# A decode block that streams a KV cache: transposed PV, an aligned load ring, an earlier wo half and a shorter ending

## The chip, the cores and the metric

The kernel runs on one core of a Trainium2 chip. The metric is device time in microseconds, the median over several executions. Ratios are the mean time of one kernel's runs over that of the kernel before in the same rounds, so they are not quite the ratio of the medians quoted.

## The reference

One token passes through an adaLN-conditioned block: modulation from `c`, a layer norm, attention with a cached K and V (32 query heads, 8 KV heads, 32768 positions, head size 128), an output projection, a second layer norm, and a ReLU MLP.

```python
mod = (_silu(c) @ w_mod).reshape(c.shape[0], 6, 1, -1)
sa, ca, ga, sb, cb, gb = ...
h = _layernorm(x) * (1 + ca) + sa
q = (h @ wq)...;  scores = q . k * Dh**-0.5;  p = softmax(scores);  o = p @ v
x = x + ga * (o.reshape(B, Sq, Hq * Dh) @ wo)
h = _layernorm(x) * (1 + cb) + sb
x = x + gb * (jnp.maximum(h @ w1, 0) @ w2)
```

K and V are 134 MB of the 149.4 MB that the kernel must read, so it is a streaming problem: nothing is used twice.

## The kernel before

All large inputs come through one ring of eight 16 KB slots a partition, on one DMA queue, in a fixed order. Each load of 2 MB is 128 packets of 16 KB (the trace has 8704 of them for 68 such loads), and its semaphore counts to 16. The completion records show sixteen separate increments, and the page counts 16 DMA engines, so each increment is read here as the end of one engine's share of the load. The ring follows the pool of constants in memory.

```python
    const = ctx.enter_context(tc.tile_pool(name="const", bufs=1))
    ring = ctx.enter_context(tc.tile_pool(name="ring", bufs=8))
    ktpool = ctx.enter_context(tc.tile_pool(name="ktpool", bufs=3))
    spool = ctx.enter_context(tc.tile_pool(name="spool", bufs=2))
...
    stream = [("wm", 0), ("wm", 1), ("wq", 0), ("wq", 1)]
    stream += [("k", 0, u) for u in range(NTILE)]
    for g in range(Hkv):
        for u in range(NTILE):
            if g + 1 < Hkv:
                stream.append(("k", g + 1, u))
            stream.append(("v", g, u))
    stream += [("wo", b) for b in range(NHALF)]
    stream += [("w1",), ("w2a",), ("w2b",)]
```

PV holds a slice of the probabilities stationary and streams V, 16 matmuls of 512 columns for each 2 MB tile. It leaves four partial sums side by side, which `gather` adds up.

```python
    def pv(g, u):
        if u == 0:
            o_tiles[g] = ps_o.tile([16, 4 * Dh], F32, tag="o", name="o_ps")
        o_ps, PT_g = o_tiles[g], PT_tiles[g]
        Vsb = need(("v", g, u))
        G, s0 = u // 2, 4 * (u % 2)
        for j in range(16):
            c0 = (16 * G + j) * 32 + 4 * s0
            nc.tensor.matmul(
                o_ps[:], lhsT=PT_g[:, c0:c0 + 16],
                rhs=Vsb[:].rearrange("p (s j) d -> p s j d", j=16)[:, :, j, :],
                start=(u == 0 and j == 0), stop=(u == NTILE - 1 and j == 15),
            )

    def gather(g):

        b, gl = divmod(g, GH)
        X = spool.tile([16, 4 * Dh], F32, tag="X", name="X")
        nc.scalar.copy(out=X[:], in_=o_tiles.pop(g)[:])
        for s in range(4):
            nc.tensor.matmul(
                acc[b][:, 0:Dh], lhsT=osel[:, gl, s, :], rhs=X[:, s * Dh:(s + 1) * Dh],
                start=False, stop=(gl == GH - 1 and s == 3), skip_group_check=True,
            )
```

The layer norm works on a transposed vector (128 x 4). Its middle is a matmul with ones that sums over partitions (0.59 us in the ending's timeline).

```python
    def layernorm_T(src_T, dst_T, shiftT, scaleT, tagp):
        stat_in = const.tile([P, 2], F32, name=f"stat_in_{tagp}")
        junk = const.tile([P, KT], F32, name=f"junk_{tagp}")
        nc.vector.tensor_scalar(
            out=junk[:], in0=src_T, scalar1=1.0 / D, scalar2=None,
            op0=ALU.mult, op1=ALU.add, accum_out=stat_in[:, 0:1],
        )
        nc.vector.scalar_tensor_tensor(
            out=junk[:], in0=src_T, scalar=1.0 / D, in1=src_T,
            op0=ALU.mult, op1=ALU.mult, accum_out=stat_in[:, 1:2],
        )
        stat_ps = small_ps([P, 2], f"stat_ps_{tagp}")
        nc.tensor.matmul(stat_ps[:], lhsT=ones_f[:], rhs=stat_in[:], start=True, stop=True)
        st = const.tile([P, 2], F32, name=f"st_{tagp}")
        nc.vector.tensor_copy(out=st[:], in_=stat_ps[:])
        negvar = const.tile([P, 1], F32, name=f"negvar_{tagp}")
        nc.vector.scalar_tensor_tensor(
            out=negvar[:], in0=st[:, 0:1], scalar=st[:, 0:1], in1=st[:, 1:2],
            op0=ALU.mult, op1=ALU.subtract,
        )
        std = const.tile([P, 1], F32, name=f"std_{tagp}")
        nc.scalar.activation(out=std[:], in_=negvar[:], func=ACT.Sqrt, bias=eps_t[:], scale=-1.0)
        rstd = const.tile([P, 1], F32, name=f"rstd_{tagp}")
        nc.vector.reciprocal(out=rstd[:], in_=std[:])
        xn = const.tile([P, KT], F32, name=f"xn_{tagp}")
        nc.vector.tensor_scalar(
            out=xn[:], in0=src_T, scalar1=st[:, 0:1], scalar2=rstd[:],
            op0=ALU.subtract, op1=ALU.mult,
        )
        t1 = const.tile([P, KT], F32, name=f"t1_{tagp}")
        nc.vector.scalar_tensor_tensor(
            out=t1[:], in0=scaleT, scalar=1.0, in1=xn[:], op0=ALU.add, op1=ALU.mult,
        )
        nc.vector.tensor_tensor(out=dst_T, in0=t1[:], in1=shiftT, op=ALU.add)
```

The main loop and the ending. `project(b)` multiplies by one half of wo (2 MB each, 64 matmuls of one column). `rows4` turns the residual `x1` into row form with 16 small fp32 matmuls (32 passes in the profile, 1.16 us) and a copy on VectorE (0.29 us); `normalise(b)` forms `o2` out of four heads' groups.

```python
    build_qbd(0)
    for u in range(NTILE):
        scores(0, u)
    softmax(0)
    for g in range(Hkv):
        if g + 1 < Hkv:
            build_qbd(g + 1)
        for u in range(NTILE):
            if g + 1 < Hkv:
                scores(g + 1, u)
            pv(g, u)
        PT_tiles.pop(g)
        if g + 1 < Hkv:
            softmax(g + 1)
        gather(g)
        if g % GH == GH - 1:
            normalise(g // GH)
    for b in range(NHALF):
        project(b)
...
    x1T = const.tile([P, KT], F32)
    nc.vector.tensor_tensor(out=x1T[:], in0=attnT_ps[:], in1=modT_sb[:, 2 * KT:3 * KT], op=ALU.mult)
    nc.vector.tensor_tensor(out=x1T[:], in0=x1T[:], in1=xT[:], op=ALU.add)
    h2T = const.tile([P, KT], BF16)
    layernorm_T(x1T[:], h2T[:], modT_sb[:, 3 * KT:4 * KT], modT_sb[:, 4 * KT:5 * KT], "ln2")

    x1_rows = rows4(x1T[:], "x1_rows")

    w1_sb = need(("w1",))
    w1_f = w1_sb[:].rearrange("p kt (a m b) -> p kt a b m", m=P, b=FB)
    ...  # 56 matmuls with w1 into hidT_ps
    hidT = const.tile([P, FT], BF16)
    nc.scalar.activation(out=hidT[:], in_=hidT_ps[:], func=ACT.Relu)
    ffn_ps = small_ps([P, P], "ffn_ps")
    nc.vector.memset(ffn_ps[:], 0.0)
    for part, base, n in (("w2a", 0, FA - 1), ("w2b", FA - 1, 1)):
        w2_sb = need((part,))
        for a in range(n):
            for b in range(FB):
                ft = (base + a) * FB + b
                for i in range(KT):
                    nc.tensor.matmul(
                        ffn_ps[32 * i:32 * i + 1, :], lhsT=hidT[:, ft:ft + 1],
                        rhs=w2_sb[:, a, b, i * P:(i + 1) * P], start=False, stop=(ft == FT - 1),
                        skip_group_check=True,
                    )
```

## Time and profile before

| | value | where read |
|---|---|---|
| time | 362.34 us (361.85 to 362.76), the three runs that the prediction had; 362.1 us with a fourth in the rounds of the result | runs |
| profiled span | 360.1 us | page |
| PE, PE weight loads, VectorE busy | 79%, 34%, 50% | page, part 1 |
| DMA rate, middle slices | 420 to 435 GB/s | page, part 2 |
| step from one landing of a 2 MB tile to the next | 4.894 us | completion records in the trace |

The page of the kernel before: its DMA rows, one digit or number for each fortieth of the span, then its DMA queues (packets, MB, share of the 16 engines' span) and the chain of waits that ended last.

```profile
DMA  8999999999999999999999999999999999999992
GB/s 302 428 430 430 431 423 426 428 431 426 426 431 428 428 424 431 428 426 430 428 427 428 431 421 428 431 424 428 431 430 424 426 435 420 430 431 428 424 404 92
...
q1 hardware_dynamic: 11160, 149.43, 98.0%
q8 instruction: 13, 0.21, 0.2%
...
DMA 86%; DVE 6%; issue 5%; PE 2%; DVEq 0%
```

The stream never pauses between the first slice and the last two. Note q8: the page calls its kind "instruction", and its 13 packets are read here as the fetching of the program itself. The completion records below show that it takes time from the engines that carry the data, about 1.5 us a packet.

The table of DMA issues says how long after its issue a load landed (columns: transfer, queue, count, KB, median us).

```profile
Vsb<-in_A_v_cache_dram SPq DMA_DIRECT2D x32, 2048.0 KB, 33.9
```

A load lands 33.9 us after issue and a tile takes 4.9 us, so about seven loads are always queued. A slot freed earlier buys nothing (with the ring aligned, the step was 4.862 us with the old PV in run 3 and 4.864 us with the new); only the rate of the stream, and what comes after its end, count.

PV in the groups of instructions (engine, operation, shape, count, then busy us and mean ns of one, then idle time before it):

```profile
L371 PE MATMUL o_ps<-Vsb,PT_g 128*16 128x512 bf16 x512 | 117.9, 385 | 1.1 <-DVE PT_g L352 1.0
```

The end of the kernel, from the timeline (start us, duration us, engine, line, operation, count, and in brackets the idle time before and what ended it):

```profile
346.75 2.29 PE L414 MATMUL attnT_ps<-o_sb,wo_sb 128*128 128x1 bf16 x64 [1.36 <-DMA wo_sb<-in_A_wo_dram]
...
350.97 0.29 ACT L202 ACTIVATE std_ln<-negvar_ln,eps_t 128x1 f32<-128x1 f32 x1 [8.58 <-DVE negvar_ln L197]
...
351.61 0.29 DVE L250 COPY x_rows_sb<-x_rows_ps 128x128 f32<-128x128 f32 x1 [0.67 <-PE x_rows_ps L245]
351.82 0.15 DVE L204 RECIPROCAL rstd_ln<-std_ln 128x1 f32<-128x1 f32 x1
...
352.75 1.63 PE L455 MATMUL hidT_ps<-h2T,w_sb 128*128 128x1 bf16 x56 [1.17 <-DVE h2T L214]
...
355.01 1.45 PE L469 MATMUL ffn_ps<-w2a_sb,hidT 128*1 128x128 bf16 x48 [0.63 <-DMA w2a_sb<-in_B_w_dram]
356.25 0.43 PE L469 MATMUL ffn_ps<-w2b_sb,hidT 128*1 128x128 bf16 x8
```

wo's second half waited for its DMA; the matmuls of w2 waited for theirs.

The page shows only the last of a transfer's sixteen increments. The trace has all; these are the sixteen times (us, sorted) of the last load, w2's last piece, in the kernel before:

```
352.1 352.2 352.3 352.4 352.6 352.8 353.0 353.7 353.9 353.9 354.0 354.1 355.3 355.3 355.4 355.5
```

The engines finish 3.4 us apart, in three groups 1.4 us apart: seven, five and four engines. The records of the loads before it, laid beside the packets of the instruction queues, show how this came about. After each packet of q8, in that load or the next, one engine and only one falls back by about 1.5 us, and it stays back. These are two loads around the packet at 60.5 us (landing of the fastest engine, then how far behind it each engine is, sorted; us):

```
59.2  0.0 0.2 0.2 0.2 0.3 0.3 0.4 0.4 0.4 0.5 0.5 0.6 0.6 1.2 1.9 2.0
64.1  0.0 0.2 0.2 0.2 0.3 0.3 0.4 0.4 0.4 0.5 0.6 0.6 1.2 2.0 2.0 2.1
```

An engine that was about 0.5 us behind is now 2.1 us behind. Twelve of the 13 packets were sent before the stream ended. The first eight hit eight different engines that were up with the rest; the next four hit engines that had been hit once. That makes four engines with one fetch and four with two. The fifth engine of the middle group had none: two of the four 8 KB packets of q14 (at 50.4 and 297.3 us) are each followed by a step of about 1.0 us on an engine that ends in this group.

### The profile page before, as it was taken

The numbers are of one execution on the slowest core, as the hardware profiler recorded it, in microseconds if no ns is written. First come the engines' busy times: TensorE is split into PE (matmuls) and PEld (weight loads), VectorE is DVE, ScalarE is ACT, GpSimd is POOL, SyncE is SP. The second block draws the span as 40 slices with busy tenths as digits, with TensorE's granted clock in tenths as the row PEclk, the third lists the DMA queues.
The fourth block names the chain that finished last, engine by engine and source line by source line (L and its number), as shares of the span: only waits on it lengthen the run. The fifth ranks groups of instructions, "written<-read, shape, count | busy, mean of one in ns | idle before, by whom it ended". The sixth has DMA issues, their size and how long they took to land.

```text
span 360.1 us, 3889 instructions
## 1 busy us (share of the span) xinstructions
PE 283.2 (79%) x1680; PEld 123.2 (34%) x1680; DVE 180.3 (50%) x193; ACT 31.6 (9%) x73; POOL 9.4 (3%) x15
## 2 busy tenths in 40 slices
PE   0547876987997889777977889886976799788964
PEld 0542332433333334323332323333432333333363
DVE  2239976555644465556554474446555474431021
ACT  1022012003000110003000300012000200011100
POOL 9100000000000000000000000000000000000000
PEclk9999998999699989989999989989998869999965
DMA  8999999999999999999999999999999999999992
GB/s 302 428 430 430 431 423 426 428 431 426 426 431 428 428 424 431 428 426 430 428 427 428 431 421 428 431 424 428 431 430 424 426 435 420 430 431 428 424 404 92
DMA packets 11465, 149.68 MB, mean 416 GB/s; under 512 B 1464, under 2 KB 1464, under 8 KB 2360
## 3 DMA queue, kind: packets, MB, share of 16 engines
q1 hardware_dynamic: 11160, 149.43, 98.0%
q8 instruction: 13, 0.21, 0.2%
q10 hardware_dynamic: 288, 0.00, 0.0%
q14 instruction: 4, 0.03, 0.0%
HBM read 149.42 MB, written 0.00 MB: 415 GB/s over the span
## 4 chain that ended last, share of the span: by engine, by line
DMA 86%; DVE 6%; issue 5%; PE 2%; DVEq 0%
DMA Ksb<-in_A_k_cache_dram 76%; DMA w2a_sb<-in_B_w_dram 9%; DVE KTt L305 6%; DMA xc_bf<-in_c_dram 2%; PE o_ps L371 1%; PE S_ps L314 1%; PE ffn_ps L469 0%; DVE S_g L320 0%; DVE o_rows L475 0%; DVE o_bf L477 0%; DVEq L305 0%; PE mT_ps L330 0%
## 5 line engine op out<-in xcount | busy, mean ns | idle before, releaser
L305 DVE STREAM_TRANSPOSE KTt<-Ksb 128x2048 f32<-128x2048 f32 x64 | 144.5, 2287 | 61.2 <-DMA Ksb<-in_A_k_cache_dram 61.2
L314 PE MATMUL S_ps<-KTt,qbd 128*128 128x512 bf16 x512 | 133.7, 411 | 34.4 <-DVE KTt L305 33.5
L371 PE MATMUL o_ps<-Vsb,PT_g 128*16 128x512 bf16 x512 | 117.9, 385 | 1.1 <-DVE PT_g L352 1.0
L314 PEld LDWEIGHTS <-qbd 128*128 128x128 bf16 x512 | 51.2, 103 | 111.8 <-issue 67.8
L371 PEld LDWEIGHTS <-PT_g 128*16 128x16 bf16 x512 | 44.2, 91 | 72.5 <-issue 15.5
L320 DVE TENSOR_SCALAR_CACHE_REDUCE S_g<-S_ps 128x512 f32<-128x512 f32 x16 | 11.0, 686 | 42.4 <-PE S_ps L314 42.4
L284 ACT COPY qbd<-qrep_sb 32x128 bf16<-32x128 bf16 x32 | 9.4, 295 | 179.5 <-PE S_ps L314 178.4
L381 ACT COPY X<-o_ps 16x512 f32<-16x512 f32 x8 | 4.6, 575 | 100.3 <-PE o_ps L371 100.3
L231 PE MATMUL modT_ps<-siluT,wm_sb 128*128 128x1 bf16 x96 | 3.3, 172 | 12.3 <-DVE siluT L223 12.3
L332 DVE TENSOR_REDUCE Mrow<-mT_ps 1x4 f32<-1x128 f32 x8 | 2.2, 279 | 20.6 <-PE mT_ps L330 20.6
L352 DVE STREAM_TRANSPOSE PT_g<-P_g 128x1024 bf16<-128x1024 bf16 x8 | 9.7, 1211 | 5.4 <-ACT P_g L347 5.3
L383 PE MATMUL oh_ps<-X,osel 16*16 16x128 f32 x64 | 10.2, 305 | 1.1 <-ACT X L381 1.1
L358 PE MATMUL oh_ps<-l_g,lsel 128*16 128x1 f32 x16 | 1.6, 171 | 11.4 <-ACT P_g L347 11.4
L347 ACT ACTIVATE P_g<-S_g,nbias 128x1024 bf16<-128x1024 f32 x8 | 9.2, 1148 | 0.4 <-ACT nbias L344 0.2
L394 DVE RECIPROCAL linv<-oh_ps 16x1 f32<-16x1 f32 x2 | 0.3, 134 | 15.8 <-PE oh_ps L383 15.8
L231 PEld LDWEIGHTS <-wm_sb 128*128 128x128 bf16 x96 | 3.4, 118 | 12.1 <-DMA wm_sb<-in_w_mod_dram 7.2
L262 PE MATMUL qT_ps<-hT,wq_sb 128*128 128x1 bf16 x128 | 3.7, 165 | 4.3 <-DVE hT L214 3.4
L383 PEld LDWEIGHTS oh_ps<-X,osel 16*16 16x16 f32 x64 | 5.8, 102 | 3.4 <-ACT X L381 1.8
L342 PE MATMUL Mb_ps<-ident_f,Mexp 1*128 1x1 f32 x16 | 3.0, 256 | 3.7 <-DVE Mexp L337 3.7
L414 PE MATMUL attnT_ps<-o_sb,wo_sb 128*128 128x1 bf16 x128 | 4.6, 172 | 1.4 <-DMA wo_sb<-in_A_wo_dram 1.4
L358 PEld LDWEIGHTS oh_ps<-l_g,lsel 128*16 128x16 f32 x16 | 0.9, 97 | 12.6 <-ACT P_g L347 9.7
L262 PEld LDWEIGHTS <-wq_sb 128*128 128x128 bf16 x128 | 3.6, 104 | 4.4 <-issue 3.5
(86 smaller groups left out, 60.3 us busy)
## 6 DMA issues: line engine op xcount, KB each, us to landing
Ksb<-in_A_k_cache_dram SPq DMA_DIRECT2D x32, 2048.0 KB, 34.0
Vsb<-in_A_v_cache_dram SPq DMA_DIRECT2D x32, 2048.0 KB, 33.9
wq_sb<-in_A_wq_dram SPq DMA_DIRECT2D x2, 2048.0 KB, 17.1
wo_sb<-in_A_wo_dram SPq DMA_DIRECT2D x2, 2048.0 KB, 34.2
wm_sb<-in_w_mod_dram SPq DMA_DIRECT2D x2, 1536.0 KB, 6.4
w_sb<-in_B_w_dram SPq DMA_DIRECT2D x1, 1792.0 KB, 34.0
w2a_sb<-in_B_w_dram SPq DMA_DIRECT2D x1, 1536.0 KB, 32.4
w2b_sb<-in_B_w_dram SPq DMA_DIRECT2D x1, 256.0 KB, 25.4
```

The lines of the kernel that those rows point to most:

```text
L231: nc.tensor.matmul(modT_ps[:, j * KT + ko:j * KT + ko + 1], lhsT=lhsT[:, ko, :], rhs=siluT[:, kt:kt + 1], start=(kt == 0), stop=(kt == KT ...
L262: nc.tensor.matmul(qT_ps[:, hq:hq + 1], lhsT=wq_sb[kt // 2][:, kt % 2, hq * Dh:(hq + 1) * Dh], rhs=hT[:, kt:kt + 1], start=(kt == 0), stop ...
L284: nc.scalar.copy(out=o, in_=i)
L305: nc.vector.transpose(out=KTt[:].bitcast(F32), in_=Ksb[:, 32 * half:32 * half + 32, :].rearrange("p j d -> p (j d)").bitcast(F32),)
L314: nc.tensor.matmul(S_ps[:], lhsT=qbd[g % 2][:, hp, s, :], rhs=KTv[:, 16 * sl:16 * sl + 16, h, :, par], start=(t4 == 0 and sl == 0 and hp = ...
L320: nc.vector.tensor_scalar(out=S_tiles[g][:, G, :], in0=S_ps[:], scalar1=1.0, scalar2=None, op0=ALU.mult, op1=ALU.max, accum_out=m_tiles[g] ...
L347: nc.scalar.activation(out=P_g[:], in_=S_g[:].rearrange("p g f -> p (g f)"), func=ACT.Exp, bias=nbias[:], scale=scale, accum_out=l_g[:],)
L352: nc.vector.transpose(out=PT_g[:], in_=P_g[:])
L371: nc.tensor.matmul(o_ps[:], lhsT=PT_g[:, c0:c0 + 16], rhs=Vsb[:].rearrange("p (s j) d -> p s j d", j=16)[:, :, j, :], start=(u == 0 and j ...
L381: nc.scalar.copy(out=X[:], in_=o_tiles.pop(g)[:])
L383: nc.tensor.matmul(acc[b][:, 0:Dh], lhsT=osel[:, gl, s, :], rhs=X[:, s * Dh:(s + 1) * Dh], start=False, stop=(gl == GH - 1 and s == 3), sk ...
L414: nc.tensor.matmul(attnT_ps[:, ko:ko + 1], lhsT=wo_sb[:, r, :].rearrange("p (m ko) -> p ko m", ko=KT)[:, ko, :], rhs=o2[:, r:r + 1], start ...
```

## The change

Its intent, part by part: hold V stationary so that PV's result comes out transposed and needs no gathering (four times as many matmuls, each of 4 columns); start the ring at a multiple of 256 bytes; load and use wo's first half ahead of the last V; shorten the norm; split w2 in three so that little work follows the last landing; and make the x1 rows after w1's matmuls.

The diff, cut to its core:

```diff
+
+    front = ctx.enter_context(tc.tile_pool(name="front", bufs=1))
+    mask4 = front.tile([P, 32], F32, name="mask4_sb")[:, 0:REP]
+    ring = ctx.enter_context(tc.tile_pool(name="ring", bufs=8))
     const = ctx.enter_context(tc.tile_pool(name="const", bufs=1))
-    ring = ctx.enter_context(tc.tile_pool(name="ring", bufs=8))
...
+    W2P = [(0, FA - 3), (FA - 3, 2), (FA - 1, 1)]      # w2 in pieces of 4, 2 and 1 (was 6 and 1)
...
     for g in range(Hkv):
+        if g == Hkv - 1:
+            stream.append(("wo", 0))
         for u in range(NTILE):
             if g + 1 < Hkv:
                 stream.append(("k", g + 1, u))
             stream.append(("v", g, u))
-    stream += [("wo", b) for b in range(NHALF)]
-    stream += [("w1",), ("w2a",), ("w2b",)]
+    stream += [("wo", 1), ("w1",)] + [("w2", i) for i in range(len(W2P))]
...
-    def layernorm_T(src_T, dst_T, shiftT, scaleT, tagp):
-        stat_in = const.tile([P, 2], F32, name=f"stat_in_{tagp}")
+    def layernorm_T(src_T, stat_in, dst_T, shiftT, nscaleT, tagp):
+
         junk = const.tile([P, KT], F32, name=f"junk_{tagp}")
-        nc.vector.tensor_scalar(
-            out=junk[:], in0=src_T, scalar1=1.0 / D, scalar2=None,
-            op0=ALU.mult, op1=ALU.add, accum_out=stat_in[:, 0:1],
-        )
         nc.vector.scalar_tensor_tensor(
-            out=junk[:], in0=src_T, scalar=1.0 / D, in1=src_T,
+            out=junk[:], in0=src_T, scalar=1.0, in1=src_T,
             op0=ALU.mult, op1=ALU.mult, accum_out=stat_in[:, 1:2],
         )
         stat_ps = small_ps([P, 2], f"stat_ps_{tagp}")
-        nc.tensor.matmul(stat_ps[:], lhsT=ones_f[:], rhs=stat_in[:], start=True, stop=True)
+        nc.tensor.matmul(stat_ps[:], lhsT=onesD_f[:], rhs=stat_in[:], start=True, stop=True)
+        nu = const.tile([P, KT], F32, name=f"nu_{tagp}")
+        nc.vector.tensor_tensor(out=nu[:], in0=src_T, in1=nscaleT, op=ALU.mult)
...
+        cen = const.tile([P, KT], F32, name=f"cen_{tagp}")
+        nc.vector.scalar_tensor_tensor(
+            out=cen[:], in0=nscaleT, scalar=st[:, 0:1], in1=nu[:], op0=ALU.mult, op1=ALU.subtract,
+        )
         rstd = const.tile([P, 1], F32, name=f"rstd_{tagp}")
         nc.vector.reciprocal(out=rstd[:], in_=std[:])
-        xn = const.tile([P, KT], F32, name=f"xn_{tagp}")
-        nc.vector.tensor_scalar(
-            out=xn[:], in0=src_T, scalar1=st[:, 0:1], scalar2=rstd[:],
-            op0=ALU.subtract, op1=ALU.mult,
-        )
-        t1 = const.tile([P, KT], F32, name=f"t1_{tagp}")
         nc.vector.scalar_tensor_tensor(
-            out=t1[:], in0=scaleT, scalar=1.0, in1=xn[:], op0=ALU.add, op1=ALU.mult,
-        )
-        nc.vector.tensor_tensor(out=dst_T, in0=t1[:], in1=shiftT, op=ALU.add)
+            out=dst_T, in0=cen[:], scalar=rstd[:], in1=shiftT, op0=ALU.mult, op1=ALU.add,
+        )
 
 
...
+        Lexp = spool.tile([P, REP], F32, tag="Lexp", name="Lexp")
+        nc.vector.tensor_scalar(out=Lexp[:], in0=mask4, scalar1=l_g[:], scalar2=None, op0=ALU.mult)
+        L_ps = small_ps([P, REP], "L_ps")
+        nc.tensor.matmul(L_ps[:], lhsT=ones_f[:], rhs=Lexp[:], start=True, stop=True)
+        Linv = spool.tile([P, REP], F32, tag="Linv", name="Linv", bufs=3)
+        nc.vector.reciprocal(out=Linv[:], in_=L_ps[:])
+        Linv_tiles[g] = Linv
 
...
         if u == 0:
-            o_tiles[g] = ps_o.tile([16, 4 * Dh], F32, tag="o", name="o_ps")
-        o_ps, PT_g = o_tiles[g], PT_tiles[g]
+            o_tiles[g] = ps_o.tile([P, REP], F32, tag="o", name="oT_ps")
+        oT_ps, PT_g = o_tiles[g], PT_tiles[g]
         Vsb = need(("v", g, u))
         G, s0 = u // 2, 4 * (u % 2)
-        for j in range(16):
-            c0 = (16 * G + j) * 32 + 4 * s0
+        for j in range(TK):
+            c0 = (16 * G + j % 16) * 32 + REP * (s0 + j // 16)
             nc.tensor.matmul(
-                o_ps[:], lhsT=PT_g[:, c0:c0 + 16],
-                rhs=Vsb[:].rearrange("p (s j) d -> p s j d", j=16)[:, :, j, :],
-                start=(u == 0 and j == 0), stop=(u == NTILE - 1 and j == 15),
+                oT_ps[:], lhsT=Vsb[:, j, :], rhs=PT_g[:, c0:c0 + REP],
+                start=(u == 0 and j == 0), stop=(u == NTILE - 1 and j == TK - 1),
             )
 
-    def gather(g):
+    def normalise(g):
 
         b, gl = divmod(g, GH)
-        X = spool.tile([16, 4 * Dh], F32, tag="X", name="X")
-        nc.scalar.copy(out=X[:], in_=o_tiles.pop(g)[:])
-        for s in range(4):
-            nc.tensor.matmul(
-                acc[b][:, 0:Dh], lhsT=osel[:, gl, s, :], rhs=X[:, s * Dh:(s + 1) * Dh],
-                start=False, stop=(gl == GH - 1 and s == 3), skip_group_check=True,
-            )
+        o_g = oT_sb[:, REP * g:REP * (g + 1)]
+        nc.vector.tensor_tensor(out=o_g, in0=o_tiles.pop(g)[:], in1=Linv_tiles.pop(g)[:], op=ALU.mult)
+        nc.vector.tensor_tensor(
+            out=oA[b][:, REP * gl:REP * (gl + 1), :],
+            in0=o_g.unsqueeze(2).to_broadcast([P, REP, CH]),
+            in1=cmask[:].unsqueeze(1).to_broadcast([P, REP, CH]), op=ALU.mult,
+        )
 
...
+    def spread(b):
+
         o2_ps = small_ps([P, RH], "o2_ps")
-        for cc in range(CH):
-            nc.tensor.matmul(
-                o2_ps[:], lhsT=esel[:, cc, :, :].rearrange("h x y -> h (x y)"),
-                rhs=oh[:, RH * cc:RH * (cc + 1)], start=(cc == 0), stop=(cc == CH - 1),
-            )
+        nc.tensor.matmul(
+            o2_ps[:], lhsT=oA[b][:].rearrange("p h c -> p (h c)"), rhs=rsel[:], start=True, stop=True,
+        )
...
-        gather(g)
+        normalise(g)
         if g % GH == GH - 1:
-            normalise(g // GH)
-    for b in range(NHALF):
-        project(b)
-
-
+            spread(g // GH)
+        if g == Hkv - 2:
+            project(0)
+    project(1)
+
+
+    stat2 = const.tile([P, 2], F32)
     x1T = const.tile([P, KT], F32)
     nc.vector.tensor_tensor(out=x1T[:], in0=attnT_ps[:], in1=modT_sb[:, 2 * KT:3 * KT], op=ALU.mult)
-    nc.vector.tensor_tensor(out=x1T[:], in0=x1T[:], in1=xT[:], op=ALU.add)
+    nc.vector.scalar_tensor_tensor(
+        out=x1T[:], in0=x1T[:], scalar=1.0, in1=xT[:], op0=ALU.mult, op1=ALU.add, accum_out=stat2[:, 0:1],
+    )
     h2T = const.tile([P, KT], BF16)
-    layernorm_T(x1T[:], h2T[:], modT_sb[:, 3 * KT:4 * KT], modT_sb[:, 4 * KT:5 * KT], "ln2")
-
-    x1_rows = rows4(x1T[:], "x1_rows")
+    layernorm_T(x1T[:], stat2, h2T[:], modT_sb[:, 3 * KT:4 * KT], ncb[:], "ln2")
 
...
     nc.scalar.activation(out=hidT[:], in_=hidT_ps[:], func=ACT.Relu)
+    x1_rows = rows4(x1T[:], "x1_rows")
```

The cuts leave out the constants: the old selection matrices go, and a few small masks come.

More of the change, by code (lines that the diff above doesn't have):

```diff
@@ L101, in load @@
             src = w1_v
-        elif kind == "w2a":
-            t = ring.tile([P, FA - 1, FB, D], BF16, tag="slot", name="w2a_sb")
-            src = w2_v[:, 0:FA - 1]
-        else:
-            t = ring.tile([P, 1, FB, D], BF16, tag="slot", name="w2b_sb")
-            src = w2_v[:, FA - 1:FA]
+        else:
+            a0, n = W2P[key[1]]
+            t = ring.tile([P, n, FB, D], BF16, tag="slot", name="w2_sb")
+            src = w2_v[:, a0:a0 + n]
         i = nc.sync.dma_start(out=t[:], in_=src)
@@ L150 @@
     nc.gpsimd.memset(qbd[1][:], 0.0)
-    lsel = const.tile([P, GH, HH], F32)
-    nc.gpsimd.memset(lsel[:], 0.0)
-    for gl in range(GH):
-        nc.vector.tensor_reduce(
-            out=lsel[:, gl, REP * gl:REP * gl + REP],
-            in_=ident_f[:].rearrange("p (x q) -> p q x", q=REP), op=ALU.add, axis=AX.X,
-        )
-    osel = const.tile([16, GH, 4, HH], F32)
-    nc.gpsimd.memset(osel[:], 0.0)
-    for gl in range(GH):
-        nc.vector.tensor_copy(
-            out=osel[:, gl, :, REP * gl:REP * gl + REP],
-            in_=ident_f[0:16, 0:16].rearrange("p (s q) -> p s q", q=REP),
-        )
-    esel = const.tile([HH, CH, HH, CH], BF16)
-    nc.gpsimd.memset(esel[:], 0.0)
-    for cc in range(CH):
-        nc.vector.tensor_copy(out=esel[:, cc, :, cc], in_=ident_bf[0:HH, 0:HH])
+    onesD_f = const.tile([P, P], F32)
+    nc.gpsimd.memset(onesD_f[:], 1.0 / D)
+    nc.vector.tensor_reduce(
+        out=mask4, in_=ident_f[:].rearrange("p (x q) -> p q x", q=REP), op=ALU.add, axis=AX.X,
+    )
+    cmask = const.tile([P, CH], F32)
+    nc.vector.tensor_reduce(
+        out=cmask[:], in_=ident_f[:].rearrange("p (c r) -> p c r", r=RH), op=ALU.add, axis=AX.X,
+    )
+    rsel_f = const.tile([P, RH], F32)
+    nc.vector.tensor_reduce(
+        out=rsel_f[:], in_=ident_f[:].rearrange("p (c r) -> p r c", r=RH), op=ALU.add, axis=AX.X,
+    )
+    rsel = const.tile([P, RH], BF16)
+    nc.vector.tensor_copy(out=rsel[:], in_=rsel_f[:])
+    oT_sb = const.tile([P, Hq], BF16)
+    oA = [const.tile([P, HH, CH], BF16, name=f"oA{i}") for i in range(NHALF)]
     cT = const.tile([P, KT], F32)
@@ L202, in layernorm_T @@
         nc.scalar.activation(out=std[:], in_=negvar[:], func=ACT.Sqrt, bias=eps_t[:], scale=-1.0)
+        cen = const.tile([P, KT], F32, name=f"cen_{tagp}")
+        nc.vector.scalar_tensor_tensor(
+            out=cen[:], in0=nscaleT, scalar=st[:, 0:1], in1=nu[:], op0=ALU.mult, op1=ALU.subtract,
+        )
         rstd = const.tile([P, 1], F32, name=f"rstd_{tagp}")
         nc.vector.reciprocal(out=rstd[:], in_=std[:])
-        xn = const.tile([P, KT], F32, name=f"xn_{tagp}")
-        nc.vector.tensor_scalar(
-            out=xn[:], in0=src_T, scalar1=st[:, 0:1], scalar2=rstd[:],
-            op0=ALU.subtract, op1=ALU.mult,
-        )
-        t1 = const.tile([P, KT], F32, name=f"t1_{tagp}")
-        nc.vector.scalar_tensor_tensor(
-            out=t1[:], in0=scaleT, scalar=1.0, in1=xn[:], op0=ALU.add, op1=ALU.mult,
-        )
-        nc.vector.tensor_tensor(out=dst_T, in0=t1[:], in1=shiftT, op=ALU.add)
+        nc.vector.scalar_tensor_tensor(
+            out=dst_T, in0=cen[:], scalar=rstd[:], in1=shiftT, op0=ALU.mult, op1=ALU.add,
+        )
     e_t = const.tile([P, KT], F32)
@@ L255 @@
     hT = const.tile([P, KT], BF16)
-    layernorm_T(xT[:], hT[:], modT_sb[:, 0:KT], modT_sb[:, KT:2 * KT], "ln1")
+    stat1 = const.tile([P, 2], F32)
+    nc.vector.reduce_sum(out=stat1[:, 0:1], in_=xT[:], axis=AX.X)
+    nca = const.tile([P, KT], F32)
+    nc.vector.tensor_scalar(
+        out=nca[:], in0=modT_sb[:, KT:2 * KT], scalar1=-1.0, scalar2=-1.0, op0=ALU.mult, op1=ALU.add,
+    )
+    ncb = const.tile([P, KT], F32)
+    nc.vector.tensor_scalar(
+        out=ncb[:], in0=modT_sb[:, 4 * KT:5 * KT], scalar1=-1.0, scalar2=-1.0, op0=ALU.mult, op1=ALU.add,
+    )
+    layernorm_T(xT[:], stat1, hT[:], modT_sb[:, 0:KT], nca[:], "ln1")
     wq_sb = [need(("wq", 0)), need(("wq", 1))]
@@ L287 @@
     S_tiles, m_tiles, S_ps_tiles = {}, {}, {}
-    PT_tiles = {}
+    PT_tiles, Linv_tiles = {}, {}
     o_tiles = {}
-    acc = {}
     def scores(g, u):
@@ L353, in softmax @@
         PT_tiles[g] = PT_g
-        b, gl = divmod(g, GH)
-        if gl == 0:
-            acc[b] = ps_acc.tile([HH, Dh + 1], F32, tag="oh", name="oh_ps")
-            nc.vector.memset(acc[b][:], 0.0)
-        nc.tensor.matmul(
-            acc[b][:, Dh:Dh + 1], lhsT=lsel[:, gl, :], rhs=l_g[:],
-            start=False, stop=(gl == GH - 1), skip_group_check=True,
-        )
+        Lexp = spool.tile([P, REP], F32, tag="Lexp", name="Lexp")
+        nc.vector.tensor_scalar(out=Lexp[:], in0=mask4, scalar1=l_g[:], scalar2=None, op0=ALU.mult)
@@ L375, in pv @@
             )
-    def gather(g):
+    def normalise(g):
         b, gl = divmod(g, GH)
-        X = spool.tile([16, 4 * Dh], F32, tag="X", name="X")
-        nc.scalar.copy(out=X[:], in_=o_tiles.pop(g)[:])
-        for s in range(4):
-            nc.tensor.matmul(
-                acc[b][:, 0:Dh], lhsT=osel[:, gl, s, :], rhs=X[:, s * Dh:(s + 1) * Dh],
-                start=False, stop=(gl == GH - 1 and s == 3), skip_group_check=True,
-            )
-    o2_tiles = {}
-    def normalise(b):
-        oh_ps = acc.pop(b)
-        linv = spool.tile([HH, 1], F32, tag="linv", name="linv")
-        nc.vector.reciprocal(out=linv[:], in_=oh_ps[:, Dh:Dh + 1])
-        oh = spool.tile([HH, Dh], BF16, tag="oh_sb", name="oh_sb")
-        nc.vector.tensor_scalar(
-            out=oh[:], in0=oh_ps[:, 0:Dh], scalar1=linv[:], scalar2=None, op0=ALU.mult,
-        )
-        o2_ps = small_ps([P, RH], "o2_ps")
-        for cc in range(CH):
-            nc.tensor.matmul(
-                o2_ps[:], lhsT=esel[:, cc, :, :].rearrange("h x y -> h (x y)"),
-                rhs=oh[:, RH * cc:RH * (cc + 1)], start=(cc == 0), stop=(cc == CH - 1),
-            )
+        o_g = oT_sb[:, REP * g:REP * (g + 1)]
[4 more added lines that the diff above has]
+            in1=cmask[:].unsqueeze(1).to_broadcast([P, REP, CH]), op=ALU.mult,
+        )
@@ L405, in normalise @@
+    o2_tiles = {}
+    def spread(b):
+        o2_ps = small_ps([P, RH], "o2_ps")
+        nc.tensor.matmul(
+            o2_ps[:], lhsT=oA[b][:].rearrange("p h c -> p (h c)"), rhs=rsel[:], start=True, stop=True,
+        )
         o2 = spool.tile([P, RH], BF16, tag="o2_sb", name="o2_sb")
@@ L434 @@
             softmax(g + 1)
-        gather(g)
+        normalise(g)
         if g % GH == GH - 1:
-            normalise(g // GH)
-    for b in range(NHALF):
-        project(b)
+            spread(g // GH)
[3 more added lines that the diff above has]
+    stat2 = const.tile([P, 2], F32)
     x1T = const.tile([P, KT], F32)
     nc.vector.tensor_tensor(out=x1T[:], in0=attnT_ps[:], in1=modT_sb[:, 2 * KT:3 * KT], op=ALU.mult)
-    nc.vector.tensor_tensor(out=x1T[:], in0=x1T[:], in1=xT[:], op=ALU.add)
+    nc.vector.scalar_tensor_tensor(
+        out=x1T[:], in0=x1T[:], scalar=1.0, in1=xT[:], op0=ALU.mult, op1=ALU.add, accum_out=stat2[:, 0:1],
+    )
     h2T = const.tile([P, KT], BF16)
-    layernorm_T(x1T[:], h2T[:], modT_sb[:, 3 * KT:4 * KT], modT_sb[:, 4 * KT:5 * KT], "ln2")
-    x1_rows = rows4(x1T[:], "x1_rows")
+    layernorm_T(x1T[:], stat2, h2T[:], modT_sb[:, 3 * KT:4 * KT], ncb[:], "ln2")
     w1_sb = need(("w1",))
@@ L460 @@
     nc.scalar.activation(out=hidT[:], in_=hidT_ps[:], func=ACT.Relu)
+    x1_rows = rows4(x1T[:], "x1_rows")
     ffn_ps = small_ps([P, P], "ffn_ps")
     nc.vector.memset(ffn_ps[:], 0.0)
-    for part, base, n in (("w2a", 0, FA - 1), ("w2b", FA - 1, 1)):
-        w2_sb = need((part,))
+    for part, (base, n) in enumerate(W2P):
+        w2_sb = need(("w2", part))
         for a in range(n):
```

## The prediction

> **What bounds the kernel now.** The DMA stream. The page's DMA row is 8 tenths or more in 39 of 40 slices, and steady slices carry 420 to 431 GB/s. The table of DMA issues shows 2048 KB tiles landing a median 34 us after issue, about seven tiles deep at 4.89 us each, so the queue never runs dry. DMA has 86% of the chain of waits. PE is busy 79%, but faster PE work only frees ring slots early. Time before: 362.34 us, profiled span 360.1 us.
>
> **What the change does, costed.**
>
> 1. *PV.* 512 matmuls of 385 ns (117.9 us in the groups) become 2048 weight loads of 128x128 with 4 columns. From groups of that form in the timeline (64 in 2.29 us, 126 in 3.52 us) I estimate 28 to 36 ns each, 60 to 75 us in all: off the critical path, worth nothing. But PE's program grows from 3055 to 6090 instructions. The instruction queue moved 13 packets of 16 KB before; I estimate 25 after. In the trace's completion records a fetch puts one DMA engine 1.4 us behind, and a transfer lands when its slowest engine does: the sixteen increments of the last load spread from 352.1 to 355.5 us. I expect that spread to grow from 3.4 to about 4.5 us: **+1.1 us**.
>
> 2. *Ring alignment.* In the built programs the ring starts at byte 41600 before (128 past a multiple of 256), 16640 after (a multiple). The 16 KB packets took 611 to 613 ns. [...]
>
> 3. *wo's first half earlier.* The second half lands after the same bytes as before (346.7 us), and its matmuls already waited 1.4 us for it. The last V lands 4.9 us later; its PV (about 2.3 us) and the short normalise still end before wo's second half. **0**.
>
> 4. *Tail.* From wo's second half: 2.3 us of matmuls, then 3.7 us to h2T before; one reduction and two of three final vector steps go, about -0.65 us. But the x1 row matmuls (1.16 us) now stand between w1's and w2's in PE's order. w2 in three pieces leaves only 8 matmuls behind the last landing. Net **-0.3 us**.
>
> **Sum:** 362.34 + 1.1 - 2.7 - 0.3 = 360.4 us. Range 357.9 to 363.2 us. Chances: faster by over 2% 0.04, within 2% 0.94, slower by over 2% 0.02.
>
> **What would show it.** [...] Instruction queue near 25 packets and a wider spread of the last landing: the fetch cost. Groups: PV below 80 us. Timeline: project's second half still waits for wo, w1's matmuls start 3.1 us after project ends instead of 3.7, and the last w2 matmuls follow the last landing by under 1 us. Chain of waits: still over 80% DMA.
>
> **What would make it wrong.** [...] fetches piling on one engine late in the stream; a last PV slower than 4 us, pushing the whole tail; PE stalling on its own instruction fetches.

The sum came to 360.4 us, and one of its terms is cut: item 2's -2.7 us for the ring's alignment. The sum counts it: 362.34 + 1.1 for the fetches - 2.7 for the alignment - 0.3 for the ending.

## More of the kernel before

One line here matters later: the standard deviation was done at 351.26 us, but the reciprocal that needs it started at 351.82 us. In VectorE's program the copy of the x1 rows stood ahead of it, and VectorE sat idle for 0.67 us until the row matmuls were done.

## The result

The changed kernel took 360.25 us (360.0 to 360.49, 4 runs) against 362.1 us (361.75 to 362.76, 4 runs) for the one before, a ratio of 0.9947 with a 95% interval of 0.993 to 0.9964. The forecast was 360.4 us. The interval says that the change is 0.4 to 0.7% faster.

The page of the changed kernel, the same rows as before:

```profile
DMA  7999999999999999999999999999999999999993
GB/s 302 428 434 423 430 437 432 417 435 432 434 421 437 428 426 432 434 424 432 434 429 424 432 429 435 426 426 432 428 435 427 423 435 434 426 426 435 426 413 119
...
q1 hardware_dynamic: 11176, 149.43, 98.0%
q8 instruction: 24, 0.39, 0.4%
...
DMA 77%; DVE 11%; PE 10%; issue 1%; ACT 0%; DVEq 0%
```

The slices are too coarse to show a rate change of under 1%, but they lean higher, and the instruction queue has gone from 13 packets to 24, while PE's program went from 3055 to 6090 instructions. PV in the groups, with its weight loads:

```profile
L374 PE MATMUL oT_ps<-PT_g,Vsb 128*128 128x4 bf16 x2048 | 56.6, 164 | 9.5 <-DMA Vsb<-in_A_v_cache_dram 5.1
L374 PEld LDWEIGHTS <-Vsb 128*128 128x128 bf16 x2048 | 56.3, 97 | 16.8 <-DMA Vsb<-in_A_v_cache_dram 5.4
```

PV's busy time halved, from 117.9 to 56.6 us. The mean record of one is 164 ns, but 56.6 us over 2048 is 27.6 ns each, so the records overlap; the last 64 of them take 1.86 us. PE now waits for V: 5.1 us of its idle time before these matmuls ended with a landing of V. The granted TensorE clock over the span fell from 0.93 to 0.77, and the score matmuls went from 411 to 475 ns. No cost of that is seen in the ending, where the 64 matmuls of wo's second half take 2.29 us and w1's 56 take 1.63 us in both kernels; why the clock fell was not tested. The table of DMA issues still shows a full queue:

```profile
Vsb<-in_A_v_cache_dram SPq DMA_DIRECT2D x32, 2048.0 KB, 34.5
```

The end of the kernel, timeline:

```profile
345.75 2.29 PE L407 MATMUL attnT_ps<-o_sb,wo_sb 128*128 128x1 bf16 x64 [2.29 <-DMA wo_sb<-in_A_wo_dram]
...
349.78 0.29 ACT L200 ACTIVATE std_ln<-negvar_ln,eps_t 128x1 f32<-128x1 f32 x1 [23.57 <-DVE negvar_ln L195]
...
350.11 0.16 DVE L206 RECIPROCAL rstd_ln<-std_ln 128x1 f32<-128x1 f32 x1 [0.23 <-ACT std_ln L200]
...
350.58 1.63 PE L450 MATMUL hidT_ps<-h2T,w_sb 128*128 128x1 bf16 x56 [1.28 <-DVE h2T L207]
...
353.07 1.78 PE L465 MATMUL ffn_ps<-w_sb,hidT 128*1 128x128 bf16 x50
```

The reciprocal now follows the standard deviation at once. From the start of wo's second half to the end of w2's matmuls it is 9.1 us (345.75 to 354.85), where it was 9.9 us (346.75 to 356.68).

The sixteen increments of the last load in the changed kernel:

```
349.9 350.0 350.1 350.2 350.3 350.6 350.6 351.7 352.9 354.0 354.1 354.3 354.3 354.3 354.3 354.4
```

These give the whole difference. The span is the landing of the fastest engine, plus the spread to the slowest, plus what follows the last landing:

| | before | after | difference |
|---|---|---|---|
| fastest engine's last landing | 352.10 | 349.94 | -2.2 |
| spread to the slowest | 3.41 | 4.50 | +1.1 |
| from the last landing to the end | 4.59 | 3.78 | -0.8 |
| span | 360.10 | 358.22 | -1.9 |

The prediction's three terms were -2.7, +1.1 and -0.3. Whether each of them has the cause that the prediction named is what the experiments ask.

### The profile page after: what moved, and what is told of

It reads as the page before. It is cut to its first block, busy times and chain, and to the rows that moved or that the text cites. A ratio compares the mean times of both kernels' runs of the same rounds, so it can differ in the third digit from the quotient of the medians.

```text
span 358.2 us, 6817 instructions
## 1 busy us (share of the span) xinstructions
PE 237.5 (66%) x3138; PEld 136.9 (38%) x3138; DVE 184.5 (52%) x207; ACT 27.0 (8%) x65; POOL 8.3 (2%) x13
## 4 chain that ended last, share of the span: by engine, by line
DMA 77%; DVE 11%; PE 10%; issue 1%; ACT 0%; DVEq 0%
DMA Ksb<-in_A_k_cache_dram 67%; DVE KTt L309 9%; DMA wo_sb<-in_A_wo_dram 9%; PE S_ps L318 6%; PE oT_ps L374 1%; DMA xc_bf<-in_c_dram 1%; PE attnT_ps L407 1%; PE ffn_ps L465 0%; PE hidT_ps L450 0%; ACT P_g L351 0%; DVE PT_g L356 0%; PE x_rows_ps L240 0%; DVE S_g L324 0%; PE stat_ps_ln L189 0%; PE L_ps L361 0%
## 5 line engine op out<-in xcount | busy, mean ns | idle before, releaser
L318 PE MATMUL S_ps<-KTt,qbd 128*128 128x512 bf16 x512 | 159.1, 475 | 59.8 <-DVE KTt L309 58.9
L318 PEld LDWEIGHTS <-qbd 128*128 128x128 bf16 x512 | 59.3, 117 | 148.5 <-issue 117.8
L374 PE MATMUL oT_ps<-PT_g,Vsb 128*128 128x4 bf16 x2048 | 56.6, 164 | 9.5 <-DMA Vsb<-in_A_v_cache_dram 5.1
L374 PEld LDWEIGHTS <-Vsb 128*128 128x128 bf16 x2048 | 56.3, 97 | 16.8 <-DMA Vsb<-in_A_v_cache_dram 5.4
L361 PE MATMUL L_ps<-Lexp,ones_f 128*128 128x4 f32 x16 | 4.5, 351 | 21.1 <-DVE Lexp L359 21.1
L361 PEld LDWEIGHTS L_ps<-Lexp,ones_f 128*128 128x128 f32 x16 | 4.0, 311 | 21.5 <-issue 21.5
L348 ACT ACTIVATE nbias<-Mb_ps 128x1 f32<-128x1 f32 x8 | 1.4, 172 | 90.2 <-PE Mb_ps L346 90.2
L174 DVE CAST cT<-xc_bf 128x4 f32<-128x4 bf16 x1 | 3.8, 3764 | 4.2 <-DMA xc_bf<-in_c_dram 4.2
L346 PEld LDWEIGHTS Mb_ps<-ident_f,Mexp 1*128 1x128 f32 x16 | 2.8, 217 | 7.4 <-DVE Mexp L341 7.0
L407 PEld LDWEIGHTS <-wo_sb 128*128 128x128 bf16 x128 | 4.6, 119 | 2.4 <-DMA wo_sb<-in_A_wo_dram 2.4
```

Source lines behind the costliest of these rows:

```text
L318: nc.tensor.matmul(S_ps[:], lhsT=qbd[g % 2][:, hp, s, :], rhs=KTv[:, 16 * sl:16 * sl + 16, h, :, par], start=(t4 == 0 and sl == 0 and hp = ...
L346: nc.tensor.matmul(Mb_ps[:], lhsT=Mexp[:], rhs=ident_f[0:1, 0:1], start=True, stop=True)
L361: nc.tensor.matmul(L_ps[:], lhsT=ones_f[:], rhs=Lexp[:], start=True, stop=True)
L374: nc.tensor.matmul(oT_ps[:], lhsT=Vsb[:, j, :], rhs=PT_g[:, c0:c0 + REP], start=(u == 0 and j == 0), stop=(u == NTILE - 1 and j == TK - 1),)
L407: nc.tensor.matmul(attnT_ps[:, ko:ko + 1], lhsT=wo_sb[:, r, :].rearrange("p (m ko) -> p ko m", ko=KT)[:, ko, :], rhs=o2[:, r:r + 1], start ...
```

## The experiments

Theory: the aligned ring speeds up every engine; PE's longer program costs fetches that put some engines behind; the ending is shorter. Rivals: the lighter PV made the stream faster; fetches are hidden; alignment is a coincidence of placement. Here is what the completion records of all useful runs show (step: mean of 64 tiles on the engine that is first; times in us).

| run | ring mod 256 | step | q8 packets | fastest, last landing | slowest | span | median time |
|---|---|---|---|---|---|---|---|
| before | 128 | 4.894 | 13 | 352.1 | 355.5 | 360.1 | 362.1 |
| changed | 0 | 4.864 | 24 | 349.9 | 354.4 | 358.2 | 360.25 |
| before, aligned | 0 | 4.863 | 13 | 349.8 | 353.2 | 359.2 | 359.74 |
| changed, 128 off | 128 | 4.893 | 24 | 352.2 | 357.1 | 360.8 | 362.72 |
| changed, 64 off | 64 | 4.896 | 24 | 352.3 | 357.8 | 361.6 | 363.38 (one run) |
| changed, 192 off | 192 | 4.897 | 24 | 352.3 | 357.6 | 361.4 | 363.21 (one run) |
| old PV, wo late | 0 | 4.862 | 13 | 349.9 | 353.0 | 358.1 | 359.49 |
| changed, wo late | 0 | 4.864 | 24 | 349.8 | 354.5 | 358.3 | 360.19 |
| before, 1280 GpSimd memsets | 128 | 4.895 | 13 (+10 on q14) | 352.1 | 358.6 | 363.2 | 365.34 |
| changed, old ending | 0 | 4.862 | 24 | 349.8 | 354.4 | 359.0 | 361.01 |
| changed, rows early | 0 | 4.865 | 24 | 350.0 | 354.6 | 358.4 | 360.19 |
| last group new | 0 | 4.865 | 14 | 349.9 | 353.4 | 357.2 | 358.84 |

### 1 and 2. Alignment alone, and alignment taken back

The kernel before, with a small tile in front of the pool of constants:

```diff
+    front = ctx.enter_context(tc.tile_pool(name="front", bufs=1))
+    pad = front.tile([P, 32], F32, name="pad_sb")
+    nc.vector.memset(pad[:, 0:1], 0.0)
     const = ctx.enter_context(tc.tile_pool(name="const", bufs=1))
```

> The kernel before with only a 128-byte tile put in front, so that the ring starts at a multiple of 256 bytes. Alignment theory: the completion step of one 2 MB tile on an unhurt DMA engine falls from 4.893 to 4.855 us, the fastest engine's last landing moves from 352.1 to about 349.9 us, instruction fetches stay at 13 packets and the spread near 3.4 us, so the time falls by 2.0 to 2.7 us to 359.4 to 360.1 us. Rival (the lighter PE work of the new PV made the stream faster): step stays 4.893 us, time stays at 362.1 us.

Measured: 359.74 us, ratio 0.994 (0.9919 to 0.9961). The step fell from 4.894 to 4.863 us with PE's work untouched. This one small tile gains 2.3 us, more than the whole change does (360.25 us).

The changed kernel with the front tile made 128 bytes longer:

```diff
-    mask4 = front.tile([P, 32], F32, name="mask4_sb")[:, 0:REP]
+    mask4 = front.tile([P, 64], F32, name="mask4_sb")[:, 0:REP]
```

> The changed kernel with its ring moved 128 bytes off again, nothing else. Alignment theory: step back to 4.893 us, time up by 2.2 to 2.7 us, to 362.4 to 363.0 us. Rival (alignment does nothing, PV and tail did it): step and time as in the changed kernel, 360.25 us.

Measured: 362.72 us, ratio 1.0015 (1.0 to 1.003). The step went back to 4.893 us. Without its alignment the change is worth nothing, or a little less: the spread is 4.9 us where the kernel before has 3.4, and the shorter ending (3.8 us behind the last landing in place of 4.6) gives back only part of that.

The first of these also has a warning. One of its four runs, the profiled one, took 361.02 us, the others 359.49 to 359.90. Its timeline at the last PV:

```profile
325.83 15.67 PE L374 MATMUL o_ps<-Vsb,PT_g 128*16 128x512 bf16 x64
...
344.11 4.42 PE L417 MATMUL attnT_ps<-o_sb,wo_sb 128*128 128x1 bf16 x128
```

In the kernel before, the same 64 matmuls took 14.02 us at a granted clock of 1.00 (the same stretch here: 0.89), and there was a wait between the two halves of wo. Here 128 matmuls run in one piece: with the stream 2 us earlier, the old PV has become the last thing to finish. How late it is goes with the clock of the run: the three shorter runs were granted 0.93 to 0.94 over the span, this one 0.922.

### 3. The old PV in the changed kernel

All code of the old PV, gathering and normalising put back, and wo's first half in its old place; everything else as changed.

```diff
-                oT_ps[:], lhsT=Vsb[:, j, :], rhs=PT_g[:, c0:c0 + REP],        # 64 per tile
+                o_ps[:], lhsT=PT_g[:, c0:c0 + 16],                            # 16 per tile
+                rhs=Vsb[:].rearrange("p (s j) d -> p s j d", j=16)[:, :, j, :],
 ... (with lsel, osel, esel, gather and normalise(b) of the kernel before)
```

> The changed kernel with the old PV (512 wide matmuls, gather, old normalise) and the old place of wo's first half; ring aligned, short norm, three w2 pieces and row order kept. Fetch theory: the instruction queue falls from 24 to 13 packets, the spread of the last landing from 4.5 to about 3.4 us, and the time by about 1.1 us to 359.2 us. Rival (the new PV relieves PE and that is worth time): the time rises to 361 us or more.

Measured: 359.49 us (358.87 to 359.93). Fetches back at 13 packets, spread 3.1 us, last landing 353.0 us, 1.4 us earlier than in the changed kernel. Only 0.8 us of it reached the median time. In the profiled run (359.93 us) PE was late again, as in the run above:

```profile
324.84 16.08 PE L379 MATMUL o_ps<-Vsb,PT_g 128*16 128x512 bf16 x64
...
343.54 4.43 PE L422 MATMUL attnT_ps<-o_sb,wo_sb 128*128 128x1 bf16 x128
```

The four runs fall in two pairs: 359.9 us at a granted clock of 0.917, and 358.9 and 359.1 us at 0.93. In the second pair 1.2 to 1.4 us of the 1.4 arrived. So the new PV costs fetches all along, and it is worth something in one place: at the last V.

### 4. More instructions on PE: a failed test

1536 one-element matmuls were added to the kernel before, behind those of PV.

```diff
+            for _ in range(3):
+                nc.tensor.matmul(
+                    attnT_full[0:1, KT:KT + 1], lhsT=ident_bf[0:1, 0:1], rhs=ident_bf[0:1, 0:1],
+                    start=True, stop=True, skip_group_check=True,
+                )
```

> The kernel before with 1536 one-element matmuls added behind the PV matmuls, which nothing reads: PE's program grows to 6127 instructions, the ring stays 128 off. Fetch theory: about 25 packets in the instruction queue, the spread of the last landing grows from 3.4 to about 4.5 us, and the time rises by about 1 us to 363.2 us. Rival (instruction count does not matter as long as PE has slack): 362.1 us, spread as before. If PE runs out of slack the groups would show PE near 360 us busy, and the run would not count for either.

Measured: 395.68 us. The result says nothing of fetches. The added matmuls depended on nothing, so the scheduler put all of them between 12 and 84 us, most of them ahead of the first scores, and the stream ran out of free slots (page of this run):

```profile
GB/s 313 427 426 429 418 23 5 369 275 285 395 208 429 434 429 426 428 424 429 426 431 426 425 429 429 428 428 428 428 428 426 428 426 427 426 428 433 426 409 115
```

While the stream stood still, engines that were behind caught up (the spread of one load fell from 2.0 us at 50 us to 0.4 us at 123 us), so even the last spread (3.1 us with 25 packets) can't be used.

### 5 and 9. More instructions on an idle engine

GpSimd has nothing to do after the first 10 us. It got one-element memsets of a tile that nobody reads: 2560 at first, then 1280.

```diff
+    junk_pool = const.tile([1, 1], F32, name="junk_pool")
+    for _ in range(2560):          # 1280 in the second run
+        nc.gpsimd.memset(junk_pool[:], 0.0)
```

> The fourth run did not test the fetches: the added matmuls, which depended on nothing, were run in a lump early and the stream ran dry. So here the instructions go to the idle GpSimd engine: the kernel before with 2560 one-element memsets of a tile nobody reads, issued without waits. PE, VectorE and the stream's slots are untouched. Fetch theory: about 10 packets more in the instruction queue (23), the spread of the last landing grows from 3.4 to 4.3 to 5 us, and the time rises by 0.9 to 1.6 us to 363.0 to 363.7 us. Rival (fetches are hidden, and the wider spread of the changed kernel has another cause): 362.0 us and a spread of 3.4 us.

Measured: 388.37 us, but the memsets themselves ran to 385.6 us, past the stream, so the time is theirs. The completion records were the surprise. Fifteen engines landed the last load by 355.7 us as before; one landed it at 365.0 us. The fetches that the memsets added (8 KB each, on q14) all went to the same DMA engine.

> In the run with 2560 GpSimd memsets every fetch of GpSimd's program fell on one and the same DMA engine, which ended 12.5 us behind the rest, but the memsets themselves also outlasted the stream. With 1280 of them GpSimd is done near 200 us. Fetch theory: about 10 fetches of 8 KB on that engine, 0.6 us each, so it ends about 6 us behind and the last landing moves from 355.5 to 358 to 359 us; the time rises by 2.5 to 4 us to 364.8 to 366 us, with PE, VectorE and the tile step (4.893 us) as before. Rival (the engine catches up while the others wait for slots, or fetches are hidden): 362.1 us.

Measured: 365.34 us, ratio 1.0093 (1.0078 to 1.0108). Queue lines of its page:

```profile
q8 instruction: 13, 0.21, 0.2%
q14 instruction: 14, 0.11, 0.1%
q10 hardware_dynamic: 288, 0.00, 0.0%
```

Ten packets more on q14 than the 4 of the kernel before, 0.08 MB in 149 MB. The sixteen increments of the last load:

```
352.1 352.3 352.5 352.7 352.8 352.9 353.8 353.9 353.9 353.9 353.9 354.1 355.2 355.5 355.6 358.6
```

The step is unchanged at 4.895 us, and fifteen engines end where they did. One is 6.5 us behind the first, and the whole kernel is 3.3 us longer. So these fetches were not hidden. The engine that served them did not catch up, and no other took over a part of its share: its lag grew by 0.65 us with each added packet, was 6.7 us when GpSimd had finished (197.7 us), and was 6.5 us at the end.

### 6. wo's first half back behind the last V

```diff
-        if g == Hkv - 1:
-            stream.append(("wo", 0))
-stream += [("wo", 1), ("w1",)] + ...
+stream += [("wo", 0), ("wo", 1), ("w1",)] + ...
-        if g == Hkv - 2:
-            project(0)
+    project(0)
     project(1)
```

> The changed kernel with only wo's first half put back behind the last V. The prediction's view: worth nothing, because wo's second half lands after the same bytes either way; 360.25 us within 0.3 us, and the second half's matmuls still start at its landing (345.7 us). Rival (the early half shortens the tail): up by 0.5 us or more, with both halves' 4.5 us of matmuls in a row.

Measured: 360.19 us (360.06 to 360.39), the same as the changed kernel. Timeline:

```profile
340.94 2.29 PE L405 MATMUL attnT_ps<-o_sb,wo_sb 128*128 128x1 bf16 x64 [2.28 <-DMA wo_sb<-in_A_wo_dram]
345.80 2.29 PE L405 MATMUL attnT_ps<-o_sb,wo_sb 128*128 128x1 bf16 x64 [2.58 <-DMA wo_sb<-in_A_wo_dram]
```

Both halves wait for their data. With the new PV, the order of wo and the last V is worth nothing.

### 7 and 12. How much alignment is needed

The front tile made 64 and 192 bytes longer, one look each (`[P, 48]` and `[P, 80]` in place of `[P, 32]`).

> The changed kernel with its ring 64 bytes off a multiple of 256. [...] If any start off a multiple of 256 pays the same, it is 4.893 us as at 128 off. If 64-byte starts are as good as 256-byte ones, 4.855 to 4.861 us.

> The changed kernel with its ring 192 bytes off a multiple of 256. At 64 and 128 off the tile step was 4.892 and 4.893 us. If any start off 256 pays one fixed price: 4.893 us again. [...]

Measured: median steps of 4.892 and 4.893 us, as at 128 off (4.893 us), against 4.854 to 4.862 us for aligned rings. The price is flat: at 64, 128 and 192 bytes off it is the same. Had it grown with the bytes off, it would have been half as large at 64 and one and a half times as large at 192.

### 10 and 11. The ending

The old norm, the rows and their copy in the old place, and w2 in two pieces, in the changed kernel:

```diff
-W2P = [(0, FA - 3), (FA - 3, 2), (FA - 1, 1)]
+W2P = [(0, FA - 1), (FA - 1, 1)]
 ... (layernorm_T of the kernel before, called as there)
+    x1_rows = rows4(x1T[:], "x1_rows")
     w1_sb = need(("w1",))
```

> The changed kernel with the old ending: the long norm, the x1 rows and their copy ahead of w1's matmuls, w2 in two pieces. The traces of the two kernels put the ending, from the landing of wo's second half to the last w2 matmul, at 10.0 and 9.2 us, so this version should take 361.0 us (up 0.8), of which the prediction gave the change only 0.3.

Measured: 361.01 us (360.87 to 361.16), so the ending as a whole is worth 0.8 us. The run does not part the shorter norm from the third piece of w2.

Only the rows moved back ahead of w1's matmuls:

> The changed kernel with only the x1 rows (32 matmul passes and the copy) put back ahead of w1's matmuls. Reading of the traces: there the copy, which waits for the row matmuls, stands ahead of the norm's reciprocal in VectorE's order and holds it for 0.5 us, and behind w1's matmuls the rows hold w2's for 0.9 us; the last landing of w2 (354.4 us) leaves only 0.4 us to gain. So h2T 0.5 us later after wo's matmuls (3.0 instead of 2.5 us), and the time the same within 0.3 us: 360.0 to 360.4 us. The prediction's view (moving the rows cost the change 0.35 us or more): 359.9 us or less.

Measured: 360.19 us (359.93 to 360.36), no difference. Timeline:

```profile
349.93 0.29 ACT L200 ACTIVATE std_ln<-negvar_ln,eps_t 128x1 f32<-128x1 f32 x1 [23.73 <-DVE negvar_ln L195]
350.57 0.29 DVE L245 COPY x_rows_sb<-x_rows_ps 128x128 f32<-128x128 f32 x1 [0.54 <-PE x_rows_ps L240]
350.78 0.15 DVE L206 RECIPROCAL rstd_ln<-std_ln 128x1 f32<-128x1 f32 x1
```

The copy again holds the reciprocal, 0.56 us after the standard deviation is done (0.04 us in the changed kernel). What the rows cost behind w1's matmuls, they save in front of them.

### 8. A version that beats both

The new PV for the last KV head alone, the old one for the seven before; the rows ahead of w1's matmuls but without a copy, since the last addition reads them in PSUM (0.29 us in this run's timeline, as from the copy in the kernel before); the rest as changed.

```diff
+    def pv(g, u):
+        if g < LAST:
+            return pv_wide(g, u)          # the old PV
 ... (the last block's o2_ps sums the old form of three groups and the new form of the last)
-    x1_rows = rows4(x1T[:], "x1_rows")
+    x1_rows = ps_s.tile([P, 512], F32, tag="s", name="x1_rows_ps")[:, 0:P]     # right after the norm
 ...
-    nc.vector.tensor_tensor(out=o_bf[:], in0=o_rows[:], in1=x1_rows[:], op=ALU.add)
+    nc.vector.tensor_tensor(out=o_bf[:], in0=o_rows[:], in1=x1_rows, op=ALU.add)
```

> A version meant to beat both: the changed kernel with the new PV for the last KV head alone (short tail, 3442 PE instructions) and the old one for the seven before, and with the x1 row matmuls back before w1's but without their copy (the last addition reads them in PSUM). Fetch theory and tail reading together: 14 or 15 fetch packets, spread about 3.4 us, the last landing near 353.3 us, the end under 4.0 us behind it: 359.0 us. Rival (spread has another cause): 360.1 us.

Measured: 358.84 us (358.41 to 359.14, 6 runs), ratio 0.9893 (0.9868 to 0.9918). The runs of the kernel before in that call spread more than elsewhere (361.86 to 364.25 us, median 362.3), so the medians say it better: 3.3 us below the 362.1 us that the kernel before takes in the other calls, and 1.4 us below the changed one. Timeline:

```profile
344.23 2.30 PE L482 MATMUL attnT_ps<-o_sb,wo_sb 128*128 128x1 bf16 x64 [2.29 <-DMA wo_sb<-in_A_wo_dram]
...
351.18 1.02 PE L555 MATMUL ffn_ps<-w_sb,hidT 128*1 128x128 bf16 x32 [0.39 <-DMA w_sb<-in_B_w_dram]
352.38 0.60 PE L555 MATMUL ffn_ps<-w_sb,hidT 128*1 128x128 bf16 x16 [0.17 <-DMA w_sb<-in_B_w_dram]
353.49 0.38 PE L555 MATMUL ffn_ps<-w_sb,hidT 128*1 128x128 bf16 x8 [0.52 <-DMA w_sb<-in_B_w_dram]
```

Now each piece of w2 is waited for: the kernel is bound by DMA to its last piece. 14 fetch packets for 3442 PE instructions, a spread of 3.55 us, last landing 353.45 us.

## Why the prediction was right

The forecast was 360.4 us, and 360.25 us was measured. Point by point:

1. *DMA bounds the kernel, and PE's relief is worth nothing.* Right as to the stream. The tile step followed the ring's alignment in all twelve rows of the table, whichever PV ran. "Worth nothing" needs a limit, though: once the stream is earlier, the old PV at the last V is late (runs 1 and 3), so the new PV keeps what alignment and fewer fetches would otherwise give back there (in run 3, 0.6 of 1.4 us).

2. *Fetches, +1.1 us.* Right in size and in mechanism: 24 packets for the 25 forecast, and a spread of 4.50 us for 4.5. Taking PE's instructions away brought 13 packets and 3.1 us back; adding fetches on GpSimd alone made the kernel 3.3 us longer. The records of all loads show it fetch by fetch. In the changed kernel each of the 23 packets that q8 sent before the fastest engine had finished is followed by a step of about 1.5 us on one engine: eight engines that were up with the rest, then eight that had been hit once, then seven that had been hit twice. (The 24th packet came at 352.5 us.) So PE's fetches go round eight of the sixteen engines, in turn. At the end seven of the eight are three steps behind and one is two; the engine 1.8 us behind had two packets of q14; seven are unhurt. The last landing therefore moves by one step for every eight packets, and not by a little for each. The records do not name the engine; what they show is how far behind each of the sixteen is. The exact size had some luck in it: the prediction shows no working for it, and in the two kernels 128 bytes off the same rise from 13 to 24 packets took the spread from 3.4 to 4.9 us.

3. *Alignment, -2.7 us.* The direction was right, the size was off. Measured: -2.2 us at the fastest engine, in both directions of the test. The -2.7 us was the author's estimate, and what it rested on was not shown by any run. The runs show a flat price: at 64, 128 and 192 bytes off the median step was 4.892 to 4.893 us. The mean step gives 611.7 ns a packet off and 608.0 ns aligned, at 8 packets of each engine in a 2 MB load. The recorded duration of a packet would have been a poor sign to look for: it has a median of 613 ns before and 611 ns after, more than the steps allow, so packets of one engine seem to overlap a little. The step between landings shows the rate; the duration of a packet doesn't.

4. *wo's first half earlier, 0.* Right (run 6).

5. *Tail, -0.3 us.* This term was mis-sized: -0.8 us. "One reduction and two of three final vector steps go, about -0.65 us" left out that the copy of the x1 rows had stood in VectorE's order ahead of the reciprocal and had held it for 0.56 us. Moving the rows behind w1's matmuls was booked as a cost only. From the end of wo's matmuls to w1's it became 2.5 us, not 3.1 (3.7 before). Run 11 shows that the moved rows by themselves are neutral.

6. *The chain of waits "still over 80% DMA"*: it was 77%. This sign failed, and mostly in the middle of the stream, not at its end: loads of K have 67% of the chain where they had 76%, and the K transposes and score matmuls 16% where they had 6%. The chain also leaves the stream earlier, at the landing of wo's second half, 12.5 us before the end in place of 5.2 us. The step between landings was no longer for it, so this share was a poor sign. The last w2 matmuls ended 0.4 us after the last landing, as forecast under 1 us.

The sum came out within 0.2 us because two errors, 0.5 us too much for alignment and 0.5 us too little for the ending, cancel. That closeness was luck.

Left open: why one fetch of 16 KB for PE costs an engine about 1.5 us when its own recorded duration is 0.9 to 1.1 us and a data packet of that size takes 0.61 us, while one of 8 KB costs 0.65 us with the memsets and about 1.0 us in two cases of the kernel before; why PE's fetches use these eight engines in turn and those of the memsets a single one; and why the spread at 64 and 192 bytes off (5.5 and 5.3 us, one run each) is above the 4.9 us at 128 off.

## What to carry to other kernels

When a kernel streams at the limit of its DMA engines, ask not only how many bytes it moves but which engine finishes last. In this kernel an alignment of the destination saved 3.7 ns on every packet, and a longer program cost fetches, each about 1.5 us on one engine that no other relieved. So give a form with four times the instructions only to the stage where its shorter finish counts, here the last group (358.84 us in run 8, which also drops the rows' copy, against 360.25 us). And when small work is moved out of a dependent chain, look at what it held up in the queue of its old engine: it may pay for itself. Last, test each part alone before it is packed into a larger change: here the alignment by itself was faster than the whole.
